# Keys of two batches turned on TensorE for their softmax, an identity made by VectorE, and pair 0's left rows loaded first

## The chip, the cores and the metric

The kernel runs on one core of one Trainium2 chip. The metric is the device time of one execution in microseconds (us), the median over several runs; lower is better.

## The reference

Linear attention over `q`, `k`, `v` of shape [8 batches, 8 heads, 576 rows, 64 channels], and a feed-forward block that takes the largest of three products (maxout):

```python
q_s = np.exp(q - np.max(q, axis=-1, keepdims=True))       # softmax over a row's 64 channels
q_s = q_s / (np.sum(q_s, axis=-1, keepdims=True) + 1e-09)
k_s = np.exp(k - np.max(k, axis=2, keepdims=True))        # softmax over the 576 rows, by channel
k_s = k_s / (np.sum(k_s, axis=2, keepdims=True) + 1e-09)
kv = np.einsum('bhsd,bhse->bhde', k_s, v)
x = np.einsum('bhsd,bhde->bhse', q_s, kv)                 # then [4608 rows, 512]
h = np.maximum(np.maximum(x @ w1, x @ w2), x @ w3)        # [512 -> 768], three weights
out = h @ w_out                                           # [768 -> 512]
```

The keys' softmax runs over the rows: its maximum and its sum belong to a channel, not to a row.

## The kernel before

**Engines.** TensorE (PE; its weight loads are PEld), VectorE (DVE), ScalarE (ACT), GpSimd (POOL), and SyncE (SP), which issues the DMAs.

**Units of work.** Attention goes by pairs of heads: four pairs in each of eight batches, pair n = 4b + g. A pair's 576 rows are 512 "main" rows, four to a partition, and 64 "left" rows. The feed-forward goes by chunks: chunks 0 to 7 are the main rows of one batch each, chunk 8 holds the left rows of all batches. A chunk has 18 gates (6 groups j of 128 hidden columns by 3 weights i, L611), from which come the hidden rows (L620 to L629), and 4 second products (L649).

**Precision.** Weights and activations of the feed-forward are split in two parts, high (wh, x high) and low (wl, x low); a product is three matmuls. The weights come as 64-bit numbers in 24 slices, and each slice is joined and split on chip in class `Slice`: L310 and L327, L331 on ACT, L312, L314, L315, L319 on DVE, L323 on POOL, L338 on DVE or POOL. This goes on beside attention for about the first 125 us.

**Pairs of the first two batches ("turned").** Rows lie on partitions. Keys: DVE takes maxima over a partition's rows (L402 to L404, tiles kh and km), PE transposes them (L408), DVE takes the maximum by channel (L411, kmx), PE spreads it over the partitions (L414), DVE subtracts it from the keys (L424, ke), ACT takes the exponential (L431). kv is 10 pairs of matmuls with a column of ones beside the values, which gives the sum by channel (L436, 65 columns); its reciprocal rk (L441, L442) scales kv into the block matrix bdf (L447). Queries: maximum on DVE (L470, qm), exponentials on ACT, ten small ones with a sum each (L485, qs), scaling on DVE (L509, L510, L513), transposes on PE (L554 for main rows, L558 for left rows), copies to SBUF (L563, L565). The product x (L581) goes to the high part (ACT, L584) and the low part (DVE, L586).

**Pairs of the later batches.** The maximum of the keys over partitions is taken by POOL (L421, kma), which needs a library routine loaded; queries are turned by DMA; the block matrix is split into bdh (L447) and bdl (L451).

**Memory.** PSUM has eight banks: pool pf has four (gates and second products), pool pa four (everything else). Pools of SBUF are given back and opened anew in `open_late`, `open_wo` and, when all weights are split and batch 1's x is done, `open_turn`.

**Order of the work.** Nothing is left to a scheduler: each unit is a generator of `Step`s (engine, estimated cost, what it comes after, which buffers it takes and frees), and class `Streams` plays them on estimated clocks, taking the step of smallest rank among those that can begin. Ranks come from tables: AT gives the rank of pairs 0 to 7, STEP how it grows from step to step, SLICES_AT, SLICE_HI and SLICE_LO those of the weight slices, GATES_AT those of the gates. `FIRST_LOADS` is a string of the first loads: k, q, v main rows of the next pair, K, Q, V left rows, w a weight slice. Each engine then runs its queue in that order.

**Start.** The identity for PE's transposes is made on POOL (`make_identity`); DVE and POOL fill the unused halves of buffers.

Of the kernel before, what the change touches and what calls it, by code (L numbers as in the profile page):

```python
# [9 lines left out]
F32 = mybir.dt.float32  # L10
# [163 lines left out]
def linear_attention_then_maxout_ffn(  # L174
# [49 lines left out]
    pa = ctx.enter_context(tc.tile_pool(name="pa", bufs=4, space=PSUM))  # L224
# [11 lines left out]
    bdf = [const.tile([P, P], F32, name=f"bdf{i}") for i in range(2)]  # L236
    kbuf = [const.tile([P, 2, 5, D], F32, name=f"kt{i}") for i in range(2)]
    vbuf = [const.tile([P, 2, 5, NV], F32, name=f"vt{i}") for i in range(2)]
    bdh = [const.tile([P, P], F32R, name=f"bdh{i}") for i in range(2)]
    bdl = [const.tile([P, P], F32R, name=f"bdl{i}") for i in range(2)]  # L240
    early = early_stack.enter_context(tc.tile_pool(name="early", bufs=1))
    k0 = early.tile([P, H, 5, D], F32, name="k0")
    q0 = early.tile([P, H, 5, D], F32, name="q0")
    v0 = early.tile([P, H, 5, NV], F32, name="v0")
# [4 lines left out]
    make_identity(nc, ident)  # L249
    nc.vector.memset(q0[LEFT:P, :, 4, :], 0.0)  # L250
    nc.vector.memset(k0[LEFT:P, :, 4, :], LOWEST)
    nc.vector.memset(v0[:, :, :, D:NV], 1.0)
    nc.vector.memset(v0[LEFT:P, :, 4, :], 0.0)
    for i in range(2):
        nc.gpsimd.memset(bdf[i], 0.0)
    for i in range(2):
        nc.gpsimd.memset(kbuf[i][LEFT:P, :, 4, :], LOWEST)
        nc.gpsimd.memset(qbuf[i][LEFT:P, :, 4, :], 0.0)
        nc.gpsimd.memset(vbuf[i][:, :, :, D:NV], 1.0)
        nc.gpsimd.memset(vbuf[i][LEFT:P, :, 4, :], 0.0)  # L260
        nc.gpsimd.memset(bdh[i].bitcast(F32), 0.0)
        nc.gpsimd.memset(bdl[i].bitcast(F32), 0.0)

    def main_rows(src, b, hs):
        return src[b, hs, 0:CH].rearrange("h (p s) d -> p h s d", s=4)

# [75 lines left out]
    class Pair:  # L342


        def __init__(self, b, g):
# [14 lines left out]
        def k_load(self):  # L360
            if self.b:
                prev = self.ago("ksub") if self.n >= NP + 2 else None
                yield Step("S", 0.55, [prev], kb=256)
                nc.sync.dma_start(out=self.kt[:, :, 0:4, :], in_=main_rows(k, self.b, self.hs))
                yield Step("S", 0.5, gives=("k", self.n), kb=32)
                nc.sync.dma_start(out=self.kt[0:LEFT, :, 4, :], in_=left_rows(k, self.b, self.hs))

        def v_load(self):
            if self.b:
                prev = self.ago("kv") if self.n >= NP + 2 else None  # L370
                for hh in range(2):
# [24 lines left out]
        def k_steps(self):  # L396
            n, kt = self.n, self.kt
            yield Step("V", dve(256) + dve(128) * 2, [("k", n), ("kmt", n - 1) if n else None], port="V")
            half = att.tile([P, 2, 2, D], F32, name="kh", bufs=1)
            km = att.tile([P, 2 * D], F32, name="km", bufs=1)  # L400
# [4 lines left out]
            if self.turned:  # L405
                yield Step("T", 0.25, take=[("pa", ("kmt", n))], gives=("kmt", n))
                kmt = pa.tile([P, CH], F32, name="pa")
                nc.tensor.transpose(out=kmt[:, :P], in_=km, identity=ident)  # L408
                yield Step("V", dve_reduce(P), free=[("pa", ("kmt", n))])
                kmx = att.tile([P, 1], F32, name="kmx")  # L410
# [406 lines left out]
```

## Time and profile before

| | us |
|---|---|
| median of 3 runs (718.27 to 719.03) | 718.37 |
| the profiled execution | 718.25 |
| its span | 716.5 |
| PE busy | 679.4 |
| DVE busy | 410.1 |
| ACT busy | 253.8 |
| POOL busy | 64.0 |

The times of instructions come from the profiled execution and count from the start of its span. In the rows, a name such as `pa<-ident,km` is the tile written and the tiles read; `x20` counts instructions in one row; what stands in square brackets is the engine's idle time ahead of the instruction and what ended it. "issue" means that nothing in the profile held the engine. The granted clock of PE was 0.987 on average.

### The profile page before, as it was taken

What the parts mean: (1) busy time and instruction counts of PE and PEld (TensorE: products, weight loads), DVE (VectorE), ACT (ScalarE), POOL (GpSimd) and SP (SyncE); (2) the same over time, 40 slices, a digit from 0 to 9 for tenths busy, and PEclk for the clock granted to TensorE, in tenths of its full rate; (3) what the DMA queues carried; (4) which work ended last, traced back from release to release, by engine and by line L of the source; (5) the groups of instructions that cost most, each with busy time, mean ns of one, the idle gap of its engine ahead of it and who ended that gap; (6) DMA issues with size and microseconds to landing.
All of it is one profiled execution on the core that took longest, in us unless ns stands there. A gap on an engine that the chain in (4) does not pass through costs nothing.

```text
span 716.5 us, 9658 instructions
## 1 busy us (share of the span) xinstructions
PE 679.4 (95%) x3464; PEld 543.7 (76%) x3464; DVE 410.1 (57%) x801; ACT 253.8 (35%) x596; POOL 64.0 (9%) x72
## 2 busy tenths in 40 slices
PE   2679999899999999999999999999999999999997
PEld 1357776687868887888788888888888888888886
DVE  6999999698898975684468646723222112211220
ACT  5997846434344324322332234212311111111111
POOL 2232443011100100000001000000000000000000
PEclk9888999999999999999999999999999999999999
DMA  9838315434354412530154005200100010010002
GB/s 245 229 121 267 95 62 152 145 102 115 97 154 129 108 51 70 146 109 1 40 160 111 16 28 154 77 1 20 58 0 1 15 45 1 0 45 15 1 1 59
DMA packets 83231, 58.04 MB, mean 81 GB/s; under 512 B 49136, under 2 KB 74736, under 8 KB 83184
## 3 DMA queue, kind: packets, MB, share of 16 engines
q1 hardware_dynamic: 83184, 57.44, 28.8%
q8 instruction: 27, 0.44, 0.2%
q14 instruction: 20, 0.16, 0.1%
HBM read 40.89 MB, written 9.44 MB: 70 GB/s over the span
## 4 chain that ended last, share of the span: by engine, by line
PE 84%; DVE 6%; ACT 4%; issue 2%; DMA 2%; SPq 1%; POOL 0%; DVEq 0%; ACTq 0%
PE pf L611 57%; PE pf L649 19%; PE pa L581 4%; PE pa L436 3%; ACT qe L485 2%; DMA wst<-in_moe_w_dram 1%; SPq L531 1%; DVE wx L319 1%; DVE wl L338 1%; ACT wh L331 1%; DVE tb L518 0%; DVE h_l L629 0%; DVE wx L314 0%; DMA qt<-in_q_dram 0%; DVE km L403 0%
## 5 line engine op out<-in xcount | busy, mean ns | idle before, releaser
L611 PE MATMUL pf<-x,wh 128*128 128x512 f32 x1152 | 359.5, 394 | 0.2 <-DMA wst<-in_moe_w_dram 0.2
L611 PEld LDWEIGHTS pf<-x,wh 128*128 128x128 f32 x1152 | 217.7, 189 | 47.3 <-DVE x L586 0.5
L611 PE MATMUL pf<-x,wl 128*128 128x512 f32 x576 | 230.4, 400 | 1.0 <-DVE wl L338 0.6
L623 DVE TENSOR_TENSOR m<-pf,m 128x512 f32<-128x512 f32 x108 | 74.1, 686 | 182.1 <-PE pf L611 181.3
L611 PEld LDWEIGHTS pf<-x,wl 128*128 128x128 f32 x576 | 109.2, 190 | 27.1 <-issue 1.2
L626 ACT CAST h_h<-m 128x512 fp32r<-128x512 f32 x54 | 33.5, 620 | 188.6 <-DVE m L623 188.4
L649 PE MATMUL pf<-ol,h_h 128*128 128x512 f32 x216 | 89.6, 415 | 1.5 <-ACT h_h L626 1.0
L649 PE MATMUL pf<-oh,h_l 128*128 128x512 f32 x216 | 84.7, 392 | 0.3 <-DVE h_l L629 0.3
L649 PE MATMUL pf<-oh,h_h 128*128 128x512 f32 x216 | 84.5, 391 | 0.0
L649 PEld LDWEIGHTS pf<-ol,h_h 128*128 128x128 f32 x216 | 40.7, 188 | 11.6 <-ACT h_h L626 1.5
L620 ACT COPY m<-pf 128x512 f32<-128x512 f32 x54 | 31.6, 585 | 49.5 <-PE pf L611 49.2
L629 DVE TENSOR_TENSOR h_l<-m,h_h 128x512 fp32r<-128x512 f32 x52 | 36.4, 699 | 22.1 <-ACT h_h L626 22.0
L649 PEld LDWEIGHTS pf<-oh,h_l 128*128 128x128 f32 x216 | 40.5, 188 | 9.7 <-DVE h_l L629 0.7
L421 POOL PARTITION_ALL_REDUCE kma<-km x24 | 20.8, 867 | 287.7 <-DVE ke L424 137.6
L649 PEld LDWEIGHTS pf<-oh,h_h 128*128 128x128 f32 x216 | 40.7, 188 | 7.5 <-issue 0.5
L611 PE MATMUL pf<-left,wh 128*128 128x512 f32 x144 | 44.3, 389 | 0.0
L654 ACT COPY m<-pf 128x512 f32<-128x512 f32 x36 | 21.0, 586 | 59.6 <-PE pf L649 58.8
L323 POOL TENSOR_TENSOR wst<-wx,wst 128x512 int32<-128x512 int32 x24 | 34.4, 1436 | 75.6 <-DVE wx L319 34.1
L518 DVE STREAM_TRANSPOSE tb<-qt 128x576 f32<-128x576 f32 x24 | 30.8, 1282 | 11.6 <-DMA qT<-tb 11.4
L431 ACT ACTIVATE ke<-ke 128x640 f32<-128x640 f32 x32 | 23.6, 738 | 28.0 <-DVE ke L424 27.7
L505 ACT ACTIVATE qt<-qt 128x576 f32<-128x576 f32 x24 | 16.5, 687 | 45.7 <-DVE qt L500 45.7
L611 PEld LDWEIGHTS pf<-left,wh 128*128 128x128 f32 x144 | 27.0, 188 | 5.6
(87 smaller groups left out, 671.7 us busy)
## 6 DMA issues: line engine op xcount, KB each, us to landing
wst<-in_moe_w_dram SPq DMA_DIRECT2D x18, 512.0 KB, 5.3
out_dram<-m SPq DMA_DIRECT2D x32, 256.0 KB, 2.3
kt<-in_k_dram SPq DMA_DIRECT2D x28, 256.0 KB, 3.3
vt<-in_v_dram SPq DMA_DIRECT2D x56, 128.0 KB, 3.1
qt<-in_q_dram SPq DMA_DIRECT2D x24, 288.0 KB, 3.1
qT<-tb SPq DMA_DIRECT2D x192, 36.0 KB, 1.9
wst<-in_moe_w_out_dram SPq DMA_DIRECT2D x6, 512.0 KB, 3.3
q<-in_q_dram SPq DMA_DIRECT2D x8, 256.0 KB, 4.2
```

What stands on the lines that cost most here:

```text
L323: nc.gpsimd.tensor_add(out=low.bitcast(I32), in0=x.bitcast(I32), in1=low.bitcast(I32))
L431: nc.scalar.activation(out=ke, in_=ke, func=AF.Exp)
L436: nc.tensor.matmul(out=kv[r, :NV], lhsT=ke[:, s, hh, :], rhs=self.vt[:, hh, s, :], start=(s == 0), stop=(s == 4))
L518: nc.vector.transpose(out=tb.rearrange("p e (c s) -> p s e c", s=QS), in_=self.qt.rearrange("p s (e c) -> p s e c", e=2))
L581: nc.tensor.matmul(out=xT, lhsT=l, rhs=r[:, cs], start=(i == 0), stop=(i == last))
L611: nc.tensor.matmul(out=ps, lhsT=l[:, cc, js], rhs=r, start=(cc == 0 and t == 0), stop=(cc == NC - 1 and t == 2))
L620: nc.scalar.copy(out=m, in_=self.m.pop((j, 0)))
L623: nc.vector.tensor_max(out=m, in0=self.m.pop((j, i)), in1=m)
L626: nc.scalar.copy(out=h, in_=m)
L629: unit[e].tensor_sub(out=lo, in0=m, in1=h.bitcast(F32))
L649: nc.tensor.matmul(out=po, lhsT=l, rhs=r[:, j, :], start=(j == 0 and i == 0), stop=(j == NJ - 1 and i == 2))
L654: nc.scalar.copy(out=o, in_=po)
```

## The change

**Keys of batches 0 and 1** go a new way (`k_turned`). PE transposes the pair's keys, four blocks of main rows and one of left rows, so that channels lie on partitions. DVE takes the negative maximum over the columns straight from PSUM. ACT takes the exponential with that as bias and adds up the row at the same time: the sum by channel, without a column of ones. PE transposes back, ACT or DVE copies to SBUF, and kv has 64 columns. The old path stays for the later batches (`k_plain`).

**The identity** is made by DVE: a count along the columns by doubling, its transpose, and a comparison.

**Loads.** Batch 0's keys lie by row group and are loaded by head. Pair 0's left rows (K, Q, V: 32 KB each) have their own loads, ahead; those of pairs 1 to 3 (96 KB each) come later.

**PSUM.** pa has three banks, and a new pool ps has one, cut into four quarters that are taken in turn by left transposes, kv and the 64-column x.

**The turn.** Six memsets of kt, bdh and bdl and the tiles kh, km and kma move behind `open_turn`.

**Tables.** AT, STEP, SLICE_HI, SLICE_LO, GATES_AT, ROOMS, FIRST_LOADS and Q_BY_ACT (pair 4's queries no longer have their sums from ACT) have new numbers. The core of the diff:

```diff
-Q_BY_ACT = (0, 1, 2, 3, 4, 5, 6, 7)
+FIRST_LOADS = 'kKqQvVwkqKQwvVkqwvkqvw'
+Q_BY_ACT = (0, 1, 2, 3, 5, 6, 7)
...
-    pa = ctx.enter_context(tc.tile_pool(name="pa", bufs=4, space=PSUM))
+    pa = ctx.enter_context(tc.tile_pool(name="pa", bufs=3, space=PSUM))
+    ps = ctx.enter_context(tc.tile_pool(name="ps", bufs=1, space=PSUM))
...
-    make_identity(nc, ident)
+    nc.vector.memset(count[:, 0:1], 0.0)
+    for e in range(7):
+        nc.vector.tensor_scalar_add(out=count[:, 2**e : 2 ** (e + 1)], in0=count[:, 0 : 2**e], scalar1=float(2**e))
+    nc.vector.transpose(out=turned_count, in_=count)
+    for i in range(0, P, BL):
+        nc.vector.tensor_scalar(
+            out=ident[i : i + BL, :], in0=count[i : i + BL, :], scalar1=turned_count[i : i + BL, i : i + 1],
+            scalar2=None, op0=ALU.is_equal,
+        )
...
+    quarters = ps.tile([P, 4, P], F32, name="ps")
+    small = (quarters[:, i % 4, :] for i in itertools.count())
...
+        def k_turned(self):
...
+            for s in range(4):
+                nc.tensor.transpose(
+                    out=kT[:, s * P : (s + 1) * P], in_=kt[:, s].rearrange("p h d -> p (h d)"), identity=ident
+                )
+            kTl = next(small)
+            nc.tensor.transpose(
+                out=kTl[:, :LEFT], in_=kt[:LEFT, 4].rearrange("p h d -> p (h d)"), identity=ident[:LEFT, :LEFT]
+            )
...
+            nc.vector.tensor_reduce(out=km[:, 0:1], in_=kT, op=ALU.max, axis=AX.X, negate=True)
+            nc.vector.tensor_reduce(out=km[:, 1:2], in_=kTl[:, :LEFT], op=ALU.max, axis=AX.X, negate=True)
+            nc.vector.tensor_tensor(out=km[:, 0:1], in0=km[:, 0:1], in1=km[:, 1:2], op=ALU.min)
...
+            nc.scalar.activation(out=keT[:, :CH], in_=kT, func=AF.Exp, bias=km[:, 0:1], accum_out=ks[:, 0:1])
+            nc.scalar.activation(
+                out=keT[:, CH:], in_=kTl[:, :LEFT], func=AF.Exp, bias=km[:, 0:1], accum_out=ks[:, 1:2]
+            )
...
+            for s in range(4):
+                nc.tensor.transpose(out=kep[:, s * P : (s + 1) * P], in_=keT[:, s * P : (s + 1) * P], identity=ident)
+            kel = next(small)
+            nc.tensor.transpose(out=kel[:LEFT, :], in_=keT[:, CH:], identity=ident)
...
+                (nc.scalar.copy if e == "A" else nc.vector.tensor_copy)(out=o, in_=i)
...
-            kv = pa.tile([P, CH], F32, name="pa")
+            kv = next(small)
+            nv = D if turned else NV
...
-            xT = pa.tile([P, CH], F32, name="pa")[:, :w]
+            xT = (next(small) if u else pa.tile([P, CH], F32, name="pa"))[:, :w]
...
     def open_turn():
...
+        for i in range(2):
+            nc.gpsimd.memset(kbuf[i][LEFT:P, :, 4, :], LOWEST)
+        for name, to in (("bdh", bdh), ("bdl", bdl)):
+            for i in range(2):
+                to.append(turn_pools[0].tile([P, P], F32R, name=f"{name}{i}"))
+                nc.gpsimd.memset(to[i].bitcast(F32), 0.0)
```

Lines of the new code in the rows below: L419 and L423 turn the keys, L428 to L430 take the maximum, L442 and L444 turn back, L489 is kv, L612 and L616 turn the queries (L554 and L558 before), L639 is x, L669 a gate.

The beginning of DVE's queue before; km and qm are maxima of keys and queries, wst and wx a weight slice, ident PE's identity:

```order
1 L247 MEMSET ones 128x1
2 L250 MEMSET q_101 64x8x64
3 L251 MEMSET k_100 64x8x64
4 L252 MEMSET v_102 128x40
5 L253 MEMSET v_102 64x8x65
6 L402 TENSOR_TENSOR kh<-k_100 128x256
7 L403 TENSOR_TENSOR km<-kh 128x128
8 L404 TENSOR_TENSOR km<-km,k_100 128x128
9 L470 TENSOR_REDUCE qm_131<-q_101 128x10
10 L411 TENSOR_REDUCE kmx<-pa 128x1
11 L312 TENSOR_SCALAR wx<-wst 128x512
```

The same place now:

```order
8 L254 TENSOR_SCALAR count<-count 128x32
9 L254 TENSOR_SCALAR count<-count 128x64
10 L255 STREAM_TRANSPOSE turned_count<-count 128x128
11 L257 TENSOR_SCALAR ident<-count,turned_count 32x128 x4
12 L528 TENSOR_REDUCE qm_133<-q_98 128x10
13 L428 TENSOR_REDUCE km_217<-pa 128x1
14 L429 TENSOR_REDUCE km_217<-ps 128x1
15 L430 TENSOR_TENSOR km_217<-km_217 128x1
16 L322 TENSOR_SCALAR wx<-wst 128x512
```

The fills of buffers and the three maxima of keys have gone from ahead of the first weight step; the identity and the maxima over transposed keys stand there.

PE's queue in a later batch before, between pair b's 64-column x (L581) and the next kv (L436); L611 are gates:

```order
461 L581 MATMUL pa<-q_l,bdh_93 128x64
462 L581 MATMUL pa<-q_h,bdl_95 128x64
463 L581 MATMUL pa<-q_h,bdh_93 128x64
464 L611 MATMUL pf<-x_694,wl_81 128x512
465 L611 MATMUL pf<-x_694,wh_78 128x512 x2
466 L611 MATMUL pf<-x_694,wl_81 128x512
467 L611 MATMUL pf<-x_694,wh_78 128x512 x2
468 L436 MATMUL pa<-vt_91,ke 64x65 [waits DMAHW7_49]
```

A like place now; in square brackets are the semaphores that an instruction waits for:

```order
439 L639 MATMUL ps<-q_l,bdh_1435 128x64 [waits DVE_49]
440 L639 MATMUL ps<-q_h,bdl_1439 128x64
441 L639 MATMUL ps<-q_h,bdh_1435 128x64
442 L669 MATMUL pf<-x_756,wl_82 128x512
443 L669 MATMUL pf<-x_756,wh_79 128x512 x2
444 L669 MATMUL pf<-x_756,wl_82 128x512
445 L669 MATMUL pf<-x_756,wh_79 128x512 x2
446 L489 MATMUL ps<-vt_93,ke 64x65 [waits DMAHW5_49,DVE_49]
```

The matmuls stand as before, but both x and kv write to ps and now wait for DVE, which reads the bank's last contents.

POOL's queue around the turn before, with the last weight steps (L323), the loading of a routine (the bare ISA rows) and its use:

```order
27 L323 TENSOR_TENSOR wst<-wx,wst 128x512 x11
28 L421 ISA
29 L421 ISA kma<-km 128x128 x5
30 L629 ISA
31 L629 TENSOR_TENSOR h_l<-m,h_h 128x512
32 L421 ISA
33 L421 ISA kma<-km 128x128 x2
```

And now:

```order
18 L333 TENSOR_TENSOR wst<-wx,wst 128x512 x23
19 L785 MEMSET kt_90 64x2x64
20 L785 MEMSET kt_91 64x2x64
21 L789 MEMSET bdh_1433 128x128
22 L789 MEMSET bdh_1435 128x128
23 L789 MEMSET bdl_1437 128x128
24 L789 MEMSET bdl_1439 128x128
25 L464 ISA
26 L464 ISA kma<-km 128x128 x24
```

Six memsets stand ahead of the routine, and POOL no longer changes routines for h_l.

More of the change, by code (lines that the diff above doesn't have):

```diff
@@ L6 @@
 from concourse import mybir
-from concourse.masks import make_identity
 from concourse._compat import with_exitstack
@@ L260, in linear_attention_then_maxout_ffn, with head_rows @@
         nc.gpsimd.memset(vbuf[i][LEFT:P, :, 4, :], 0.0)
-        nc.gpsimd.memset(bdh[i].bitcast(F32), 0.0)
-        nc.gpsimd.memset(bdl[i].bitcast(F32), 0.0)
     def main_rows(src, b, hs):
         return src[b, hs, 0:CH].rearrange("h (p s) d -> p h s d", s=4)
+    def head_rows(src, b, h):
+        return src[b, h, 0:CH].rearrange("(p s) d -> p s d", s=4)
     def left_rows(src, b, hs):
@@ L401, in k_steps, with k_plain @@
+        def k_plain(self):
+            n, kt = self.n, self.kt
+            yield Step("V", dve(256) + dve(128) * 2, ["turn", ("k", n), ("kmt", n - 1) if n > TURNED * NP else None], port="V")
+            half = turn_pools[0].tile([P, 2, 2, D], F32, name="kh", bufs=1)
+            km = turn_pools[0].tile([P, 2 * D], F32, name="km", bufs=1)
             kmv = km.rearrange("p (h d) -> p h d", h=2)
@@ L404, in k_steps @@
             nc.vector.tensor_max(out=kmv, in0=kmv, in1=kt[:, :, 4, :])
[L405 to L410, printed above, removed]
[L411 to L422 removed]
+            yield Step("G", 0.8, [("ksub", n - 1)], gives=("kmt", n))
+            kma = turn_pools[0].tile([P, 2 * D], F32, name="kma", bufs=1)
+            nc.gpsimd.partition_all_reduce(kma, km, P, bass_isa.ReduceOp.max)
+            yield Step("V", dve(640), take=[("ke", n)], gives=("ksub", n), port="V")
             ke = self.ke = att.tile([P, 5, 2, D], F32, name="ke")
@@ L431, in k_steps @@
             nc.scalar.activation(out=ke, in_=ke, func=AF.Exp)
-            yield Step("T", 0.9, [("v", n), self.ago("xmm", 0), self.ago("xmm", 1)], take=[("pa", ("kv", n))], free=[("ke", n)], gives=("kv", n))
-            kv = pa.tile([P, CH], F32, name="pa")
+        def k_steps(self):
+            n, turned = self.n, self.turned
+            yield from self.k_turned() if turned else self.k_plain()
+            ke = self.ke
+            last = [("ps", ("kv", n))]
+            yield Step(
+                "T", 0.9, [("v", n), self.ago("xmm", 0), self.ago("xmm", 1)], take=last, free=[("ke", n)], gives=("kv", n)
+            )
+            kv = next(small)
+            nv = D if turned else NV
             for s in range(5):
+                rows = slice(0, LEFT if turned and s == 4 else P)
                 for hh, r in enumerate(heads):
                     nc.tensor.matmul(
-                        out=kv[r, :NV], lhsT=ke[:, s, hh, :], rhs=self.vt[:, hh, s, :], start=(s == 0), stop=(s == 4)
+                        out=kv[r, :nv], lhsT=ke[rows, s, hh, :], rhs=self.vt[rows, hh, s, 0:nv],
+                        start=(s == 0), stop=(s == 4),
                     )
@@ L556, in turned_steps @@
                 )
-            qTl = pa.tile([P, CH], F32, name="pa")
+            qTl = next(small)
             nc.tensor.transpose(
@@ L679, in first_loads @@
         seen = {}
-        every = slice(0, H)
+        to, of = {"k": k0.rearrange("p s h d -> p h s d"), "q": q0, "v": v0}, {"k": k, "q": q, "v": v}
         for ch in FIRST_LOADS:
```

144 lines of the change are left out of this document (75 added, 69 removed).

## The prediction

> **What bounds the kernel now.** I read the page first: its busy line and the chain.
>
> ```profile
> PE 679.4 (95%) x3464; PEld 543.7 (76%) x3464; DVE 410.1 (57%) x801; ACT 253.8 (35%) x596; POOL 64.0 (9%) x72
> PE 84%; DVE 6%; ACT 4%; issue 2%; DMA 2%; SPq 1%; POOL 0%; DVEq 0%; ACTq 0%
> ```
>
> TensorE (PE) is busy for 679.4 of 716.5 us and carries 84% of the chain. A change can win only in the other 37 us or by taking work off PE. The table by stage shows where those 37 us lie (columns: length, busy time of PE, PEld, DVE, ACT and POOL, granted clock, DMA share, GB/s).
>
> ```profile
> 0.00:57.78 57.78, 31.11 (x185) 19.93 (x185) 49.00 (x111) 45.18 (x173) 15.28 (x29) 0.90 0.72 194
> 57.78:99.00 41.22, 41.16 (x196) 32.78 (x194) 38.13 (x70) 33.41 (x94) 16.50 (x11) 0.98 0.52 156
> 99.00:140.00 41.00, 36.92 (x217) 27.26 (x218) 33.50 (x68) 21.07 (x42) 10.29 (x8) 0.96 0.41 127
> 140.00:202.00 62.00, 60.19 (x329) 47.69 (x328) 53.94 (x111) 23.57 (x45) 7.83 (x8) 1.00 0.43 112
> 202.00:680.00 478.00, 478.00 (x2404) 389.87 (x2403) 230.64 (x439) 125.23 (x235) 14.12 (x16) 1.00 0.20 57
> 680.00:717.00 37.00, 32.02 (x142) 26.14 (x140) 4.91 (x8) 5.38 (x9) 0.00 (x0) 0.97 0.13 29
> ```
>
> PE idles 26.7 us before 57.78, then 0.1, 4.1 and 1.8 us in the next three stages, nothing from 202 to 680, and about 4.5 at the end. At 57.78 the first gate matmul runs; I call it the onset. Before it DVE is busy for 49.0 us, more than ACT (45.2) and PE (31.1). The timeline of DVE around the first maximum and the onset, and of POOL and PE beside it:
>
> ```profile
> 5.91 0.29 DVE L404 TENSOR_TENSOR km<-km,k 128x128 f32<-128x128 f32 x1 [1.61 <-DMA k<-in_k_dram]
> 6.89 0.82 DVE L470 TENSOR_REDUCE qm<-q 128x10 f32<-128x640 f32 x1 [0.69 <-DMA q<-in_q_dram]
> 9.33 0.29 DVE L411 TENSOR_REDUCE kmx<-pa 128x1 f32<-128x128 f32 x1 [1.62 <-PE pa L408]
> 56.97 0.69 DVE L586 TENSOR_TENSOR x<-pa,x 128x512 fp32r<-128x512 f32 x1
> 8.48 0.28 POOL masks.py:199 TENSOR_SCALAR_AFFINE_SELECT ident<-ident 128x128 f32<-128x128 f32 x1 [7.42 <-issue]
> 8.82 0.48 PE L408 MATMUL pa<-ident,km 128*128 128x128 f32 x1 [8.82 <-POOL ident masks.py:199]
> 57.78 0.79 PE L611 MATMUL pf<-x,wl 128*128 128x512 f32 x1
> ```
>
> POOL's identity comes at 8.8, although the keys' maxima are done by 6.2; DVE then runs almost without a gap from 9.33 until pair 3's x is split at 57.66, and the gates start 0.1 us later. So the onset is 9.33 plus what DVE has queued.
>
> **The identity and the loads.** The keys landed for 5.91 (256 KB of rows, 128 KB of left rows behind the queries). Now pair 0's keys are followed by 32 KB of left rows, then queries and 32 KB more, and the identity is built by 13 small DVE instructions from about 1 us on; the 7.42 us that POOL took leaves the path. I take the first transposes at about 6 and the first DVE maximum at about 7.0, 2.3 us before 9.33; if the keys, which now come in 256-byte pieces instead of 1-KB ones, land 1 us later for it, half of that goes (no row shows such a load of keys). But pair 0's values now stand ahead of the first weight slice, which lands later by 256 KB at the start's 194 GB/s, 1.3 us. DVE waits for it some 2 us. That eats most of the early start, unless later work absorbs it.
>
> **DVE's queue up to the onset.** Here are the groups of DVE instructions in the first 62 us, by shape.
>
> ```profile
> L470 DVE TENSOR_REDUCE qm<-q 128x10 f32<-128x640 f32 x8 | 6.5, 810 | 1.7 <-ACT qe L485 1.0 <-DMA q<-in_q_dram 0.7
> L319 DVE SCALAR_TENSOR_TENSOR wx<-wst,wx 128x512 uint32<-128x512 uint32 x9 | 6.1, 674 | 0.0
> L424 DVE TENSOR_TENSOR ke<-k,pa 128x640 f32<-128x640 f32 x4 | 3.3, 813 | 0.0
> L411 DVE TENSOR_REDUCE kmx<-pa 128x1 f32<-128x128 f32 x6 | 1.6, 273 | 1.6 <-PE pa L408 1.6
> L402 DVE TENSOR_TENSOR kh<-k 128x256 f32<-128x256 f32 x4 | 1.7, 418 | 0.7 <-DMA k<-in_k_dram 0.7
> L563 DVE COPY qf<-pa 128x512 f32<-128x512 f32 x1 | 0.7, 683 | 0.0
> ```
>
> For a pair the old key path costs DVE 1.0 us for three maxima (start to start), 0.2 for kmx and 0.73 for the subtraction (813 ns, overlapped by 0.08 with the next): 1.9 us. The new one costs a maximum over 512 columns (L470 does 640 in 0.81, so about 0.65), one over 64 and a minimum: I take 0.9; and, where DVE rather than ACT copies the turned keys back, 0.68 for 512 columns (L563's row) and 0.12 for the rest: 0.8. In the new order six maxima and three such copies stand before pair 3's split: 5.4 + 2.4 = 7.8 us. Before, five trios of maxima, six kmx and five subtractions stood there: 9.9 us. But the new tables put more else there: pair 4's queries on DVE (a subtraction at L424's 0.73, a sum at L470's price, which ACT did before), and one to two more steps of the weight split (19.4 us where 17.7 stood). My two sums over the order are 41.7 us before and 41.9 after: DVE's queue is no shorter. ACT's is equal to 0.2 us.
>
> What DVE lost to POOL was in none of these. Two maxima beside POOL's work, with the same instruction when POOL was idle:
>
> ```profile
> 51.34 1.36 POOL L323 TENSOR_TENSOR wst<-wx,wst 128x512 int32<-128x512 int32 x1 [1.94 <-ACT wh L331]
> 51.58 1.27 DVE L403 TENSOR_TENSOR km<-kh 128x128 f32<-128x128 f32 x1
> 52.78 1.29 POOL L338 TENSOR_TENSOR wl<-wst,wh 128x512 fp32r<-128x512 f32 x1
> 52.88 1.34 DVE L404 TENSOR_TENSOR km<-km,kt 128x128 f32<-128x128 f32 x1
> 4.01 0.29 DVE L403 TENSOR_TENSOR km<-kh 128x128 f32<-128x128 f32 x1
> ```
>
> 0.29 us became 1.3 beside POOL: 2 us in one pair. Added up over the instructions that ran longer than their like, DVE lost about 4.7 us from 9.33 to 57.66 and idled 1.9. The new maximum has one operand, in PSUM, as L411 has, whose row averages 273 ns against 0.29 at 9.33, where no other row is stretched; I take 3.2 us of loss after, since POOL's own work stays. [...]
>
> So the end of pair 3's split after: 7.0 + 41.9 + 3.2 + about 3.3 of waits (the weight slice, one other) = 55.4, against 57.66. **Onset: 2.0 us earlier**, bounds 0 (loss and waits as before) and 4 (weights in time). Ahead of the onset PE has 13 more groups of five transposes; even at twice the price below, 1.5 us each, these 19 us fit into its 26.7 idle ones.
>
> **PE's clock and its work after the onset.**
>
> ```profile
> 60.72 0.60 PE L554 MATMUL pa<-ident,qe 128*128 128x128 f32 x4
> 61.25 0.27 PE L558 MATMUL pa<-ident,qe 64*128 64x64 f32 x1
> 61.45 0.81 PE L436 MATMUL pa<-vt,ke 128*64 128x65 f32 x20
> ...
> 128.83 0.39 PE L649 MATMUL pf<-ol,h_h 128*128 128x512 f32 x1
> 129.06 0.39 PE L649 MATMUL pf<-oh,h_h 128*128 128x512 f32 x1
> ```
>
> A group of 4+1 transposes takes 61.45 − 60.72 = 0.73 us of warm PE, 0.15 a piece. In the new order three more such groups (15 transposes) stand behind the first gate, and four single ones of the old kind go: +2.2 − 0.6 = **+1.6 us** (1 to 2.2). The first gate matmul took 0.79 us against the 0.39 of warm ones (one every 0.23); with transposes filling PE ahead of it the clock may stand high already: **−0.5** (0 to −1).
>
> **The turn to batch 2.** There the first batch's buffers are given back and POOL loads the routine for the maximum over partitions.
>
> ```profile
> 123.53 1.31 POOL L323 TENSOR_TENSOR wst<-wx,wst 128x512 int32<-128x512 int32 x1 [2.97 <-DVE wx L319]
> 130.84 0.72 POOL L421 PARTITION_ALL_REDUCE kma<-km  x1 [6.00 <-issue]
> 133.24 0.80 PE L436 MATMUL pa<-vt,ke 128*64 128x65 f32 x20 [2.21 <-ACT ke L431]
> ```
>
> One memset of POOL, and two of its waits:
>
> ```profile
> 10.16 0.40 POOL L262 MEMSET bdl<- 128x128 f32 x1
> ```
>
> ```profile
> POOL h_l L629 <- issue: 14.1, 2, 7.1
> ```
>
> PE stands 2.21 us for this chain, and the clock falls behind it. The change puts six memsets on POOL ahead of the routine (0.40 in this row, half of it where nothing slows POOL; 1.5 in all), so that kv of the first late pair comes 12.1 instead of 10.6 us after the last split step; the new order has six more gates on PE ahead of it (6 × 0.23 = 1.4) and POOL no longer changes routines for h_l (two waits of 7.1). In the stages from 99 to 202 PE lost 4.1 + 1.8 us idle and 4% of 41 us of clock, 1.6: 7.5. After, the routine's stall and its clock, 2.2 + 1.6, should be about 1.5, and the other 3.7 us, in which PE waits for DVE's queue or for h_l, about 1.5, since the turned pairs that are left cost DVE up to 1 us less each: 3.0.
>
> **The shared bank.** kv, 64-column x and left transposes now take turns in one bank, and in the built program each waits until the last one has been read.
>
> ```profile
> 169.91 0.80 PE L436 MATMUL pa<-vt,ke 128*64 128x65 f32 x20
> 169.93 0.21 DVE L586 TENSOR_TENSOR left<-pa,left 128x64 fp32r<-128x64 f32 x1
> 365.69 0.19 PE L581 MATMUL pa<-q_l,bdh 128*128 128x64 f32 x1
> 365.75 0.58 DVE L451 SCALAR_TENSOR_TENSOR bdl<-pa,rk,bdh 64x64 fp32r<-64x64 f32 x2
> ```
>
> Before, kv could start at 169.91 though the left rows were read until 170.14, and x at 365.69 though bdl was read until 366.33: 0.2 and 0.6 us that would be waits now. Of 48 such places some ten are late by 0.2 to 0.6 in this trace, the others are on time by about 1. That is 3 us (1.5 to 4) if the spacing stays. Stalls altogether go from 7.5 to 3.0 + 3 = 6.0: **−1.5** (−5 to +1).
>
> **The sum.** The profiled execution took 718.25 (span 716.5 and 1.75 around it), 0.1 under the median of 718.37. 718.25 − 2.0 − 0.5 + 1.6 − 1.5 = 715.8.
>
> **The rivals.** *No change.* If DVE's losses stay at 4.7 and the weight slice costs the 2.3 that were won, the onset is where it was, and +1.6 on PE meets −1.5 of stalls: 718. Or each of the 15 transposes costs the 0.27 of L558's row, 4.1 − 0.5 = 3.6, and none warms the clock: 718.25 − 2.0 + 3.6 − 1.5 = 718.3. For it: the two equal sums of DVE. Against it: 7.42 us of POOL have gone, and four transposes took 0.60 together. [...] *A larger gain.* If DVE's losses vanish with the maxima that POOL stretched (3.2 us less, of which 2 reach the onset: −4) and the stalls fall twice as far (−3), 718.25 − 4 − 0.5 + 1.6 − 3 = 712.4. *Slower by the bank.* If DVE is behind by more than the 1.36 us (six gates) that lie between 64-column x and the next kv, most of the 48 places wait: at the lower price above, 48 × 0.23 = 11, where 3 are counted: 715.8 − 3 + 11 = 723.8; half of them give 718.3. For it: DVE is 54 of 62 us busy at 140 to 202, and its queue is in order. Against it: 231 of 478 busy after 202, so DVE should mostly be on time. [...] *Slower at the turn.* If DVE's lighter load doesn't bring the last split step forward, the memsets' 1.5 us and a colder clock stand against PE, at the row's size once more: 715.8 + 1.5 + 2.2 = 719.5.
>
> **How the numbers follow.** The forecast 0.40, the larger gain 0.15, no change 0.22, slower by the bank 0.13 (more than half of it above 721.5), slower at the turn 0.10. 0.2% is 1.4 us, about what a measurement of this kernel can tell from no change. Faster is the first two, 0.55; within 0.2% is no change and a bit of the bank's case, 0.23; slower the rest, 0.22. The range runs from just under the larger gain to between the two slower cases, 711.5 to 721.5, and leaves out some 0.05 below and 0.10 above.
>
> **What would show it.** Right: the identity from DVE by 4 us, the first maximum at about 7, the first gate at 55 to 56.5, PE's idle time before it near 24; a PE busy sum up by less than 4 us in the stages behind it; waits of kv or x for DVE in the ps bank of under 4 us in sum. Wrong: an onset after 57.5, waits for the weight slice above 3 us, or PE idle after 202.

## The result, and the profile after

The change made the kernel slower: a median of 722.62 us (721.42 to 724.52, 5 runs) where the kernel before had 719.03 (718.27 to 719.99, 5 runs), a ratio of 1.0051, 95% interval 1.003 to 1.0072. Measured once more, on chip 12 beside its own runs of the kernel before, the changed kernel gave 721.45, ratio 1.0042 (1.002 to 1.0064). The prediction was 715.8, faster. The profiled execution took 724.52 with a span of 722.4, the slowest of its five runs, against 718.25 and 716.5 before; so the profiles differ by 5.9 us, more than the medians (3.6).

The page of the changed kernel, its busy line and its chain:

```profile
PE 690.8 (96%) x3528; PEld 553.5 (77%) x3528; DVE 404.8 (56%) x806; ACT 256.5 (36%) x610; POOL 58.4 (8%) x68
PE 85%; DVE 6%; DMA 3%; ACT 2%; SPq 2%; issue 1%; POOL 0%; DVEq 0%; ACTq 0%
```

PE is busy for 11.4 us more and idle for 5.5 us less (31.6 of 722.4 against 37.1 of 716.5). The table by stage, with nearly the stages of before:

```profile
0.00:62.75 62.75, 41.67 (x238) 28.96 (x238) 47.73 (x118) 46.53 (x178) 16.32 (x23) 0.95 0.71 193
62.75:99.00 36.25, 36.24 (x177) 29.21 (x178) 34.27 (x67) 30.61 (x88) 11.83 (x10) 1.00 0.49 161
99.00:140.00 41.00, 39.33 (x225) 30.02 (x223) 30.18 (x60) 23.16 (x53) 11.74 (x15) 1.00 0.36 114
140.00:202.00 62.00, 60.05 (x340) 47.78 (x340) 55.83 (x117) 24.68 (x50) 5.19 (x6) 0.97 0.41 109
202.00:680.00 478.00, 475.68 (x2387) 386.50 (x2386) 230.53 (x439) 125.66 (x236) 13.34 (x16) 1.00 0.21 58
```

Between 202 and 680, where PE never idled before, it now idles 2.3 us. The prediction's onset needs a word first. The matmul at 57.78 in the kernel before is not the first gate matmul but the 37th. The first runs at 25.55:

```profile
25.55 0.50 PE L611 MATMUL pf<-x,wl 128*128 128x512 f32 x1 [0.39 <-ACT x L584]
```

The four banks of pf let four gates begin with the x of pairs 0 to 2, which is 36 matmuls; the 37th is the first that needs pair 3's x. In the changed kernel the first gate matmul runs at 29.93, and this is the 37th and the one behind it, which waits until pair 3's x is split:

```profile
61.40 0.50 PE L669 MATMUL pf<-x,wl 128*128 128x512 f32 x1
62.76 0.72 PE L669 MATMUL pf<-x,wh 128*128 128x512 f32 x2 [0.85 <-DVE x L644]
```

To add up the rest, both profiles are cut at the same point of the work, the start of the 48th of the 2,592 matmuls of gates and second products (62.7 us before, 65.1 now; by then pair 3's x is split in both), and behind it PE's idle time and its occupied time, up to the end of its last matmul, are summed from the traces:

| us | before | after | |
|---|---|---|---|
| 48th gate matmul ("48th gate" below) | 62.7 | 65.1 | +2.4 |
| PE idle behind it, first 142 us | 6.0 | 3.6 | −2.3 |
| PE idle from there on | 0.0 | 2.3 | +2.3 |
| PE occupied behind it | 643.3 | 646.8 | +3.5 |

These give +5.9, the difference of the spans. The first line differs from run to run: in a second profile of the same kernel the 48th gate came at 63.9. The waits of PE behind the onset, after:

```profile
PE ps L639 <- DVE bdl L509: 1.8, 2, 1.5
PE ps L489 <- ACT bdh L505: 1.8, 1, 1.8
PE ps L489 <- ACT ke L474: 1.7, 1, 1.7
PE pf L669 <- DVE x L644: 0.9, 1, 0.9
PE ps L489 <- DVE left L644: 0.7, 2, 0.5
```

Four of the five rows write to ps, the shared bank; one of them (L489 behind ACT's ke L474) waits for its keys and not for the bank. The bank's mechanism in the timeline, a kv (L489) of a late batch and DVE's split of the left rows ahead of it:

```profile
225.30 0.21 DVE L644 TENSOR_TENSOR left<-ps,left 128x64 fp32r<-128x64 f32 x1
225.57 0.80 PE L489 MATMUL ps<-vt,ke 128*64 128x65 f32 x20 [0.53 <-DVE left L644]
```

The reader ends at 225.51, and PE, which stood for 0.53 us, starts within 0.1 us. At the turn to batch 2 PE stands twice:

```profile
126.33 1.30 POOL L333 TENSOR_TENSOR wst<-wx,wst 128x512 int32<-128x512 int32 x1 [2.49 <-DVE wx L329]
127.69 0.34 POOL L785 MEMSET kt<- 64x128 f32 x2
128.39 0.35 POOL L789 MEMSET bdl<- 128x128 f32 x2
134.55 0.72 POOL L464 PARTITION_ALL_REDUCE kma<-km  x1 [5.82 <-issue]
```

```profile
136.96 0.80 PE L489 MATMUL ps<-vt,ke 128*64 128x65 f32 x20 [1.67 <-ACT ke L474]
141.80 0.80 PE L489 MATMUL ps<-vt,ke 128*64 128x65 f32 x20 [1.76 <-ACT bdh L505]
```

The first stop is the chain of POOL that stood there before (2.21 us then), with the memsets in it. The second is new: the second kv has its keys, but the first kv's result is still being read in the same bank (bdh is made from it).

The start, as DVE and PE saw it:

```profile
2.79 1.16 DVE L257 TENSOR_SCALAR ident<-count,turned_count 32x128 f32<-32x128 f32 x4
7.11 0.68 DVE L428 TENSOR_REDUCE km<-pa 128x1 f32<-128x512 f32 x1
10.25 0.43 DVE L322 TENSOR_SCALAR wx<-wst 128x512 uint32<-128x512 uint32 x1 [2.13 <-DMA wst<-in_moe_w_dram]
45.35 0.22 DVE L644 TENSOR_TENSOR left<-ps,left 128x64 fp32r<-128x64 f32 x1 [2.48 <-PE ps L444]
62.02 0.68 DVE L644 TENSOR_TENSOR x<-pa,x 128x512 fp32r<-128x512 f32 x1
```

The identity is ready at 4.0, the first maximum runs at 7.1 and DVE waits 2.1 us for the first weight slice, all three as forecast; but pair 3's x is split at 62.7, not 55.4.

### The profile page after: what moved, and what is told of

It is laid out like the page before. It is cut to its first block, busy times and chain, and to the rows that moved or that the text cites. A ratio compares the mean times of both kernels' runs of the same rounds, so it can differ in the third digit from the quotient of the medians.

```text
span 722.4 us, 9841 instructions
## 1 busy us (share of the span) xinstructions
PE 690.8 (96%) x3528; PEld 553.5 (77%) x3528; DVE 404.8 (56%) x806; ACT 256.5 (36%) x610; POOL 58.4 (8%) x68
## 4 chain that ended last, share of the span: by engine, by line
PE 85%; DVE 6%; DMA 3%; ACT 2%; SPq 2%; issue 1%; POOL 0%; DVEq 0%; ACTq 0%
PE pf L669 60%; PE pf L707 18%; PE ps L489 3%; PE pa L639 3%; ACT qe L543 1%; DMA kt<-in_k_dram 1%; PE ps L639 1%; DMA wst<-in_moe_w_dram 1%; SPq L589 1%; DVE ke L467 1%; PE pa L612 0%; DVE x L644 0%; DVE tb L576 0%; DMA qt<-in_q_dram 0%; SPq L757 0%
## 5 line engine op out<-in xcount | busy, mean ns | idle before, releaser
L669 PE MATMUL pf<-x,wh 128*128 128x512 f32 x1152 | 361.1, 395 | 1.1 <-DVE x L644 1.1
L669 PEld LDWEIGHTS pf<-x,wh 128*128 128x128 f32 x1152 | 218.0, 189 | 50.5 <-DVE x L644 1.7
L669 PE MATMUL pf<-x,wl 128*128 128x512 f32 x576 | 232.1, 403 | 0.9 <-ACT x L642 0.9
L669 PEld LDWEIGHTS pf<-x,wl 128*128 128x128 f32 x576 | 109.2, 190 | 26.7 <-ACT x L642 1.1
L678 ACT COPY m<-pf 128x512 f32<-128x512 f32 x54 | 31.6, 586 | 52.2 <-PE pf L669 51.9
L687 DVE TENSOR_TENSOR h_l<-m,h_h 128x512 fp32r<-128x512 f32 x54 | 38.0, 704 | 20.7 <-ACT h_h L684 20.6
L669 PE MATMUL pf<-left,wh 128*128 128x512 f32 x144 | 44.3, 389 | 0.0
L669 PEld LDWEIGHTS pf<-left,wh 128*128 128x128 f32 x144 | 27.0, 188 | 5.6
L489 PEld LDWEIGHTS ps<-vt,ke 128*64 128x64 f32 (+1 forms) x560 | 18.9, 137 | 14.8 <-issue 5.0
```

The costliest lines, as they stand in the source:

```text
L489: nc.tensor.matmul(out=kv[r, :nv], lhsT=ke[rows, s, hh, :], rhs=self.vt[rows, hh, s, 0:nv], start=(s == 0), stop=(s == 4),)
L669: nc.tensor.matmul(out=ps, lhsT=l[:, cc, js], rhs=r, start=(cc == 0 and t == 0), stop=(cc == NC - 1 and t == 2))
L678: nc.scalar.copy(out=m, in_=self.m.pop((j, 0)))
L687: unit[e].tensor_sub(out=lo, in0=m, in1=h.bitcast(F32))
```

## The experiments

Theory A: the shared bank makes the loss, by writers that wait for readers and readers that wait for the next writer. Theory B: the bank is harmless, and PE's added transposes and the longer chain of a pair cost. All ratios are to the kernel before on the same chip.

| run | what differs | median us | ratio, 95% interval | 48th gate, us | PE idle behind it, us |
|---|---|---|---|---|---|
| after | | 722.62 | 1.0051, 1.003 to 1.0072 | 65.1 | 5.9 |
| a_again | the same | 721.45 | 1.0042, 1.002 to 1.0064 | 63.9 | 6.5 |
| b_shared_bank | before, with the bank | 722.59 | 1.0038, 1.0024 to 1.0052 | 63.8 | 8.9 |
| b_shared_early | before, bank in the first two batches | 719.08 | 0.9986, 0.997 to 1.0001 | 58.8 | 6.7 |
| b_ident | before, identity by DVE | 718.99 | 0.9994, 0.9984 to 1.0005 | 62.8 | 6.7 |
| e_late_x_apart | after, late x apart | 719.12 | 0.9996, 0.998 to 1.0011 | 63.1 | 3.7 |
| e_turn_dve | and memsets on DVE | 718.21 | 0.9978, 0.9964 to 0.9992 | 63.6 | 2.5 |
| e_turn_kv | late x apart, every second kv apart | 717.97 | 0.997, 0.9957 to 0.9984 | 65.5 | 2.6 |
| e_turn_both | both | 716.43 | 0.9959, 0.9945 to 0.9973 | 64.0 | 1.5 |
| e_twice | late x apart, transposes doubled | 719.25 | 0.9996, 0.9984 to 1.0008 | 64.4 | 3.4 |
| e_x_own_bank | late x apart, early x in a bank | 720.39 | 1.0008, 0.9994 to 1.0022 | 66.0 | 4.3 |
| e_w_ahead | late x apart, first slice early | 720.82 | 1.0011, 0.9999 to 1.0023 | 63.6 | 4.6 |
| e_w_both | late x apart, two slices early | 722.66 | 1.0043, 1.0028 to 1.0058 | 62.5 | 5.1 |
| e_x_apart | x left in pa everywhere | 723.10 | 1.0044, 1.0025 to 1.0063 | 62.4 | 6.2 |
| e_same_order | four rotating banks, same order | 722.36 | 1.0046, 1.003 to 1.0061 | 69.7 | 2.3 |
| e_four_banks | the same, order laid anew | 728.10 | 1.0114, 1.0099 to 1.0129 | 73.5 | 2.3 |
| e_old_tables | late x apart, old ranks | 728.00 | 1.0104, 1.0086 to 1.0123 | 63.7 | 8.3 |

**The bank taken away altogether.** Two kernels give the small tiles whole banks of pa again, one with every instruction where the change has it, one planned anew.

```diff
-    pa = ctx.enter_context(tc.tile_pool(name="pa", bufs=3, space=PSUM))
-    ps = ctx.enter_context(tc.tile_pool(name="ps", bufs=1, space=PSUM))
+    pa = ctx.enter_context(tc.tile_pool(name="pa", bufs=4, space=PSUM))
...
-    small = (quarters[:, i % 4, :] for i in itertools.count())
+    small = (pa.tile([P, CH], F32, name="pa")[:, :P] for _ in itertools.count())
```

> The changed kernel with every instruction in its place, but the left transposes, kv and the 64-column x no longer share one bank: they and the tiles of pa rotate through four banks. Theory A (the shared bank costs: a reader waits for the last writer of the bank, a writer for its last reader, and DVE and ACT stand still ahead of the onset): the 48th gate matmul comes 2 to 5 us earlier than the 65.1 of the changed kernel, PE's 2.3 us of idle time after 207 goes, and the time falls by 3 to 7 us, to 716 to 719. Theory B (the bank is harmless; what costs is PE's added transposes and pair 0's exponential behind ten of the queries on ACT): within 1 us of the changed kernel, 48th gate at 64 to 66.

> The changed kernel with four banks in pa and none shared, and the planner told so, so that the order is laid out anew. Theory A: 715 to 719, at or under the kernel before. Theory B: 721 to 723, since the transposes stay.

Both missed theory A's time: the first met that of theory B, the second neither. In the first, PE idles nothing after the first 142 us, as A has it, and from the 48th gate to the end of the span it takes 650.9 us instead of 657.3 (3.6 of the difference is PE's idle time, 2.3 instead of 5.9; how much of the rest is PE's clock was not shown). But the 48th gate comes at 69.7, 4.6 us later, where neither theory had it. So the late waits come from the bank, and early on, in this order, four whole banks in rotation serve worse than three and a shared one. Planned anew (73.5) it is worse still. Neither kernel tells the early and the late cost apart; the next one has the late cost alone.

**The late 64-column x apart.** From batch 2 on it has banks of pa, and kv alone uses ps.

```diff
-            xT = (next(small) if u else pa.tile([P, CH], F32, name="pa"))[:, :w]
+            xT = (next(small) if u and self.turned else pa.tile([P, CH], F32, name="pa"))[:, :w]
```

> The changed kernel, but from batch 2 on the 64-column x has banks of pa, so that kv alone uses the shared bank there; the first two batches are as they are. Theory A: PE's idle time after 207 falls from 2.3 us to under 0.5 and the time by about 2 us; the onset stays at 65. Theory B: no change within 1 us.

As theory A has it. All of PE's waits behind 62 us are now these two:

```profile
PE ps L489 <- ACT ke L474: 1.9, 1, 1.9
PE ps L489 <- ACT bdh L505: 1.8, 1, 1.8
```

Every engine's order is that of the changed kernel, so nothing but the banks of the late x differs, and the kernel is level with the one before. Its profile also shows the run's part in the start: the code ahead of 130 us is the changed kernel's, and the 48th gate stands at 63.1.

**The bank in the kernel before.** Pools and small tiles as in the change; keys, identity, loads and tables as before. The planner counts the new rooms and so lays the order anew from some 38 us on, so this is the bank together with another order.

```diff
-    pa = ctx.enter_context(tc.tile_pool(name="pa", bufs=4, space=PSUM))
+    pa = ctx.enter_context(tc.tile_pool(name="pa", bufs=3, space=PSUM))
+    ps = ctx.enter_context(tc.tile_pool(name="ps", bufs=1, space=PSUM))
...
-            kv = pa.tile([P, CH], F32, name="pa")
+            kv = next(small)
...
-            qTl = pa.tile([P, CH], F32, name="pa")
+            qTl = next(small)
```

> The kernel before with only the PSUM pools of the change: three banks in pa, and left transposes of queries, kv and the 64-column x in quarters of one shared bank; keys, identity, loads and tables as before. Theory A: PE idles 2 to 4 us more after the turn, where it idled nothing, and the onset comes 1 to 4 us later; 722 to 726. Theory B: 719 to 720.

It loses 0.38%, some 2.7 us of 719.5, about what the whole change loses. PE's waits behind 207 us, of which the kernel before has none:

```profile
PE ps L440 <- DVE left L590: 1.3, 3, 0.7
PE ps L585 <- DVE bdl L455: 0.9, 2, 0.5
```

Then the same with the late x in pa (kv stays in ps); its order is that of b_shared_bank, instruction by instruction, so these two differ in the bank alone:

> The kernel before with three banks in pa and one shared bank as in the change, but with the late 64-column x in pa. If the loss of 3.1 us of the fully shared kernel (722.6) was the late waits: 719 to 720.5, no idle PE after 206, onset 1 us later at most. If the sharing costs in the first two batches: 721 to 722.5.

No late wait is left and the time is back at the kernel before's. In the first two batches the sharing, with the order laid anew (48th gate 58.8), costs the kernel before nothing that can be measured; the changed kernel puts more into the bank there.

**The identity alone, in the kernel before.**

```diff
-    make_identity(nc, ident)
+    nc.vector.memset(count[:, 0:1], 0.0)
...
+            out=ident[i : i + BL, :], in0=count[i : i + BL, :], scalar1=turned_count[i : i + BL, i : i + 1],
```

> The kernel before with its identity made by DVE and nothing else. PE's first transpose should come at about 6.3 instead of 8.8, the first kmx at 6.9 instead of 9.3. If the start sets the onset, 48th gate 1.5 to 2.5 us earlier and 716.5 to 717.5; if DVE's queue waits for its first weight slice instead, within 0.7 us of the kernel before.

The second answer. PE, and then ACT, in that kernel (L417 is the first transpose, L445 kv, L494 the exponentials of pair 0's queries, L336 a weight step, L440 the exponential of pair 0's keys):

```profile
6.53 0.47 PE L417 MATMUL pa<-ident,km 128*128 128x128 f32 x1 [6.53 <-DVE km L413]
13.85 1.35 PE L445 MATMUL pa<-v,ke 128*64 128x65 f32 x20 [5.11 <-ACT ke L440]
57.41 0.80 PE L620 MATMUL pf<-x,wl 128*128 128x512 f32 x1
```

```profile
8.04 0.35 ACT L494 ACTIVATE qe<-q,qm 128x64 f32<-128x64 f32 x1 [5.83 <-DVE qm L479]
11.37 0.63 ACT L336 ACTIVATE wst<-wst 128x512 int32<-128x512 uint32 x1
13.07 0.72 ACT L440 ACTIVATE ke<-ke 128x640 f32<-128x640 f32 x1
```

The transpose comes 2.3 us earlier (6.53 against 8.82), kv only 0.4 (13.85 against 14.25), because ACT first does ten exponentials of queries and three weight steps, and the gate behind pair 3 also 0.4 (57.41 against 57.78). The early identity alone is worth nothing that can be measured.

**The start of the changed kernel.** Four edits, all on the kernel with the late x apart: the keys' transposes issued twice (`for s in (0, 1, 2, 3, 0, 1, 2, 3)`), the early 64-column x in a bank of its own taken from the gates' four, and the order of loads (`kKqQwvVkqKQwvV...` with the first slice early, `kKqQwvVwkqKQvV...` with two).

> The kernel with the late 64-column x apart, and the four transposes of each turned pair's keys are issued twice, 32 more in all, 28 of them ahead of the 48th gate and 4 behind it. If idle PE hides them ahead of the onset, as the prediction had it: only the 4 behind cost, 0.5 us, 48th gate within 1 us of 63.1, 719 to 720. If PE's own queue has become the chain there: 0.5 to 1 us a group, 48th gate 3 to 6 us later, 722 to 726.

> The kernel with the late 64-column x apart (719.1 us, 48th gate at 63.1 in its profile), and in the first two batches the 64-column x has a bank to itself, taken from the gates' pool (three banks in place of four). Theory A, that a reader of the shared bank waits for the next writer: ACT's and DVE's waits of 1.3 to 2.6 us ahead of the casts and splits of left rows go, and pair 3's split and the 48th gate come 3 to 5 us earlier; the end then depends on what three banks cost the gates, 715 to 718 if nothing. Theory B, that the pairs' own chain sets the onset: the waits go to other places and the 48th gate stays at 62 to 64.

> The kernel with the late 64-column x apart, and the first weight slice is loaded ahead of pair 0's values. DVE's wait for that slice (2.1 to 2.4 us at 8.1) should fall to about 0.8. If DVE's queue sets the onset, it comes 1 to 1.5 us earlier and the time falls to 717.5 to 718; if the shared bank's waits set it, within 0.7 us of 719.1.

> The kernel with the late 64-column x apart, with the first two weight slices loaded ahead of where they are: the first ahead of pair 0's values, the second ahead of pair 1's keys and queries, as in the kernel before. ACT's wait of about 2 us for the second slice at 13.6 should go. If that wait sets the pace of ACT and through it the onset: 48th gate 1 to 2.5 us earlier, 717 to 718.5. If not, because pair 1's keys and queries come 2 us later instead or PE is the chain: 48th gate at 62.5 to 64.5, 719 to 721.

In all but the first the planner lays the order anew, so each is its edit together with another order. Transposes: 28 more of them ahead of the 48th gate cost 1.3 us in the profile, within the spread of profiles of equal code, and nothing in the median (719.25 against 719.12); idle PE hides them. Own bank: nearer to theory B, though with 66.0 outside its 62 to 64. The waits of DVE for the left x are gone, yet pair 3's x is split at 61.12, no earlier than in the kernels of equal code without this edit (60.70 to 63.06). The gates had a bank less, so this run doesn't clear the bank altogether. Loads: the first slice early leaves the 48th gate where it was, 63.6, and the time, 720.82, meets neither expectation. With both early it comes at 62.5, but then PE stands 2.11 us for ACT, which copies a gate's result (L678) only behind ten exponentials of queries, and the granted clock over the span is 0.988, where it is 0.991 with the late x apart: the 60th gate comes 6.7 us after the 48th instead of 2.7, and the time is 3.5 us worse. No single one of these sets the onset.

**Banks of pa for every 64-column x, and the old ranks.**

> The changed kernel with the 64-column x in the banks of pa in every batch, so that left transposes and kv alone share the bank. Theory A of the bank: as the kernel with the late x apart, and ACT's waits of 1.3 and 2.2 us and DVE's of 2.6 us ahead of the left rows go too; 48th gate 1 to 3 us earlier than 63.1, 716.5 to 718.5. Theory B, that pa's three banks then bind instead or PE's queue does: 718.5 to 721.

> The kernel with the late 64-column x apart and with the ranks of the kernel before (pairs, steps, slices, gates behind everything, pair 4's queries by ACT). If the new tables are worth something with the new key path, this is slower by 1 to 5 us, 720 to 724; if they only move work about, 718 to 720.

The order is laid anew in both, and both are slower than expected. The first is slower by 4 us than with the early x in ps, outside both theories. Its start is not the reason: pair 3's x is split at 57.1 and the 48th gate comes at 62.4. Behind it PE idles 6.2 us instead of 3.7, 3.8 of them ahead of the first late kv where it was 1.9. The granted clock over the span is 0.991 in both; the rest of the 4 us is not explained. That pa's three banks are the cause, as theory B has it, was not shown. The second shows that the tables belong to the new key path: with the old ones it is 9 us slower, though pair 3's x is split at 57.0 there too.

**The turn.** Memsets on DVE, and every second late kv in pa:

```diff
-            nc.gpsimd.memset(kbuf[i][LEFT:P, :, 4, :], LOWEST)
+            nc.vector.memset(kbuf[i][LEFT:P, :, 4, :], LOWEST)
...
-                nc.gpsimd.memset(to[i].bitcast(F32), 0.0)
+                nc.vector.memset(to[i].bitcast(F32), 0.0)
...
+            apart = not turned and n % 2 == 1
-            kv = next(small)
+            kv = pa.tile([P, CH], F32, name="pa") if apart else next(small)
```

> The kernel with the late 64-column x apart, with the six memsets at the turn on DVE instead of POOL. POOL's routine is then asked for 1.0 us earlier; if that chain sets PE's wait ahead of the first late kv (1.9 us), the wait falls to about 0.9 and the time by about 1 us, to 718; if DVE's queue gives it back, 719.

> The kernel with the late 64-column x apart, with every second late kv in a bank of pa, so that one kv doesn't wait for the readers of the one before. PE's wait of 1.76 us ahead of the second late kv (released by ACT's bdh) should go, and some clock behind it: 717 to 718. If the second kv then waits for its own ke: 719.

> Both of these: 716 to 717.5 if the two waits go, under the kernel before; 718.5 to 719.5 if they are replaced.

The waits went as expected. Against the kernel with the late x apart the medians fall by 0.9 and 1.2 us, which one by one is within the noise (the intervals of the ratios overlap), and by 2.7 us for both, which is not. PE's occupied time behind the 48th gate falls with them, from 645.6 to 644.0, and its granted clock from 130 to 150 us is 1.00 instead of 0.91. In the last one PE's waits behind 62 us are these:

```profile
PE pf L670 <- DVE x L645: 0.8, 1, 0.8
PE pa L490 <- ACT ke L474: 0.7, 1, 0.7
PE ps L490 <- ACT ke L474: 0.7, 1, 0.7
```

At 716.43 us, ratio 0.9959 (0.9945 to 0.9973), it is faster than both kernels and 0.6 us from the forecast for the change. It keeps all that the change does for the keys and only undoes waits: those of the bank, and the memsets ahead of POOL's routine.

## Why the prediction was wrong, point by point

**The onset, −2.0 forecast: the step that failed.** The prediction had pair 3's split end at 55.4 instead of 57.66; it ended at 62.70, and the gate behind it came at 61.40 (61.29 in the second profile) instead of 57.78. At the 48th gate +2.4 and +1.2 of this are left: in the kernel before, five transposes and a kv stood in that stretch (60.72 to 62.18), and PE's clock was 0.83 from 57.78 to 62.75, where it is 1.00 now. That clock is the prediction's term of −0.5; 17% of 5.0 us make it −0.8, and it lies within these +2.4. What raised the clock is not shown. That transposes ahead of the gate raise it, the reason of the term, no run shows: with 28 more of them (e_twice) the granted clock from 7.11 to 62.75 us was 0.94, as without them (e_late_x_apart).

The first maximum (7.1) and DVE's work came as forecast: 41.9 + 3.2 us, and 44.2 measured between 7.1 and 62.75. Its waits did not: 3.3 forecast, 55.6 − 44.2 = 11.4 measured. Part of them are waits of readers in the shared bank:

```profile
DVE left L644 <- PE ps L444: 2.5, 1, 2.5
ACT left L642 <- PE ps L489: 3.1, 1, 3.1
ACT left L642 <- PE ps L616: 2.1, 1, 2.1
```

In the first row the left x was written by 43.12 and read at 45.35, behind PE's next writes into the bank (L444, until 45.31). With a bank of its own for the early x, in another order, these waits went, and the split came no earlier (61.12, e_x_own_bank).

The premise beneath failed: that the onset is DVE's first maximum plus DVE's queue. With the identity 2.3 us earlier in the kernel before, it moved by 0.4. The chain of work that ended at the 37th gate matmul (view --critical) shows why, although DVE was the busier engine there (49.0 us against 45.2 of ACT). In the kernel before it begins with the second weight slice, landed at 12.88, and then runs mostly through ACT; in the second profile of the changed kernel the same slice lands 2.6 us later, and the largest part is PE's. The slice's row and one of the longest behind it, before and then now:

```profile
5.84 7.04 DMA wst<-in_moe_w_dram
21.46 3.42 ACT qe L485 x20
```

```profile
9.58 5.93 DMA wst<-in_moe_w_dram
37.81 2.00 PE pa L639 x2
```

| us of the chain up to the 37th gate matmul | loads and their issue | ACT | DVE | PE |
|---|---|---|---|---|
| before | 11.8 | 23.2 | 11.1 | 6.5 |
| after, first profile | 14.5 | 15.8 | 11.8 | 16.0 |
| after, second profile | 14.2 | 18.5 | 3.2 | 22.2 |
| e_late_x_apart, the same code up to there | 22.5 | 15.4 | 10.1 | 7.6 |

DVE's first maximum of keys is on none of the first three, and DVE is never more than a fifth. A chain is inferred from semaphores and is that of one profile: in equal code its shares differ as the last three rows do. It doesn't say either what the next edit would meet: the loads, the bank and the transposes, changed one at a time, left the 48th gate between 62.5 and 66.0, where six profiles with the same code up to there have 63.1 to 65.5. In two kernels with another order (e_x_apart, e_old_tables) pair 3's split came at 57.1 and 57.0, but the 48th gate hardly earlier (62.4 and 63.7). Which edit would have brought the onset to 55.4 stays open.

**The cover for the transposes: right as far as the medians tell.** Idle PE hid 28 more of them ahead of the onset without a cost that can be measured.

**PE's work behind the onset, +1.6 (1 to 2.2) forecast: at the upper bound.** The kernel with the late x apart, which has no late waits and the same loss of clock at the turn (0.91 from 130 to 150 us in both), has 138.35 + 507.20 = 645.6 us of it against 643.3: +2.2. Beside the 15 transposes of keys, one more group of transposes of queries and 20 more matmuls of kv had been left for later (16 against 12 and 540 against 520 in the trace), and the prediction counted only the keys'. The rest of the measured 3.5, about 1.2, comes and goes with the bank's waits, in the same order of work; that it is what they do to the matmuls around them is not shown.

**The bank, 3 us in the late batches: right in mechanism, in size partly by luck.** Four waits of 0.20, 0.53, 1.47 and 0.31 us, 2.5 in sum, against about ten of 0.2 to 0.6: fewer places, and one of them longer than any that was counted. With the 1.2 us around them they make 3.7. The prediction's sign of being wrong, PE idle after 202, came true through this term, although its own example of the term lies at 365.69. Taken away, the medians fall by 2.3 to 3.5 us (719.12 against 721.45 and 722.62). The rival that had it decide the sign wanted most of 48 places late and 723.8; four places sufficed, since the gain that it was to eat did not exist; without them the kernel is level with the one before, which was the rival of no change. Each of these waits is between different quarters of one bank: the built program keeps its guards by the tile, here the bank.

**The stalls, 7.5 to 3.0 without the bank: too hopeful at the turn.** PE's idle time from 62 to 130 and from 150 to 207 fell from 1.9 and 1.8 us to 0.75 and 0.2, as forecast. At the turn it did not. The first stop lost its 2.2 us only down to 1.67. From POOL's last weight step the first late kv came 9.7 us later before (133.24 − 123.53; the prediction has 10.6) and 10.6 now (it has 12.1), so the memsets, 1.05 us and not 1.5, cost it 0.9; with them on DVE the stop falls from 1.89 to 0.76 (e_turn_dve against e_late_x_apart). The second, 1.76 us for the first kv's readers, was the bank again at a place where the prediction had not looked for it, the one where two kv follow closely (e_turn_kv). And PE's clock was no better: 0.91 from 130 to 150, as before.

**The sum by its steps**, on the first profile: 718.25 + 2.4 (onset) + 3.5 (PE work and what waits do to it) − 2.3 + 2.3 (stalls) = 724.2, against 724.52. The median was 1.1 us above the range. With the late x apart the change comes out even, and with the turn mended as well it is the 716 that was forecast, which is luck: the forecast had it from an onset that never came.

## What to carry to other kernels

In these built programs the tiles that are cut from one PSUM bank are one room, whatever the planner counts: writes waited for readers of another quarter (PE 0.53 us ahead of the kv at 225.57), and readers for writes into another (DVE 2.48 us ahead of the left x at 45.35). So put things that follow each other closely, two kv or a kv and an x, in different banks. An engine that became free earlier gained here only what the next engine in the chain could take (0.4 of 2.3 us in b_ident): the chain of the kernel before, up to the point in question, shows which engines it runs through, and the cheap test is to make that one edit alone. And in the stage where the bound engine never idled, 2.3 us of new waits counted in full (without them the medians fall by 2.3 to 3.5 us), so look there first.

## What the runs showed of the hardware

In the profiles of the kernel before and of the changed kernel PE's granted clock is at half, 0.50, in a few stretches: at the turn for 3.42 us (134.51 to 137.93 before, 142.95 to 146.37 after), and ahead of it for 6.8 us at a time (32.12 to 38.94 and 52.59 to 59.42 before, 37.14 to 43.97 after). Otherwise it is 1.00 in both from 34 to 714 us. In full work 3.42 us at half cost 1.7 us, an estimate from that. At the turn of these kernels the clock fell after two long stops close together, and not after shorter ones. Here is the stage from 130 to 150 us in the second profile of the changed kernel, with a clock of 0.83 in its second half:

```profile
130.00:150.00 20.00, 16.41 (x97) 12.77 (x96) 13.98 (x32) 7.27 (x14) 2.13 (x3) 0.91 0.44 127
140.00:150.00 10.00, 9.24 (x50) 7.48 (x51) 8.42 (x20) 2.61 (x7) 0.70 (x1) 0.83 0.50 132
```

and the first of them in the kernel with both waits mended:

```profile
130.00:150.00 20.00, 18.52 (x113) 14.60 (x112) 16.17 (x37) 9.26 (x17) 2.61 (x4) 1.00 0.46 130
```

With stops of 1.85 and 1.75 us within 5 us the clock was 17% down over the next 10 us; with stops of 0.73 and 0.74 us, and with one of each size (0.76 and 1.75 in e_turn_dve, 1.87 and 0.76 in e_turn_kv, clock 1.00 there), it stayed up. So the length of one stop didn't decide it alone between 0.7 and 1.9 us. In the kernel before, the clock fell after a single stop of 2.21 us (at half from 134.51). What else counts was not tried. Code that is the same up to the turn had its 48th gate between 63.1 and 65.5 us in six profiles: a profile's start alone can't be compared more finely than that.
